# Values loaded uncast by a hardware queue and cast on chip, with weights taking over attention buffers one by one

## The chip, the cores and the metric

One Trainium2 chip, one core. The time is the device time of one execution in microseconds (us), and the figure quoted for a kernel is the median of its runs. Most executions of one kernel agree within 1 to 2%. A run more than 1.5% above the fastest of its kernel counts as slow and stays out of the ratios. GB/s counts the bytes as they land: a float32 to float16 load is counted at half of what it reads.

## The reference

Sliding-window attention for 8 batches of 8 heads (576 rows, 64 columns), then a mixture of experts with 32 soft slots over the 4608 rows of 512.

```python
# attention: heads 0-3 see the last 32 rows, heads 4-7 every fourth of the last 128
scores = scale * np.matmul(q, k.transpose(0, 1, 3, 2))
mask_plain = (rel >= 0) & (rel < 32)
mask_dil = (rel >= 0) & (rel < 128) & (rel % 4 == 0)
attn = softmax(np.where(mask, scores, -1e9)); x = np.matmul(attn, v)
# experts
logits = x @ phi                                  # 4608 x 32
slot_input = softmax(logits, axis=0).T @ x        # 32 x 512
for e in range(8):
    slot_out[e] = np.maximum(slot_input[e] @ w1[e], 0) @ w2[e]
out = softmax(logits, axis=1) @ slot_out          # 4608 x 512
```

The inputs are float32 in HBM. q, k and v are 9.4 MB each, w1 and w2 16.8 MB each, the output 9.4 MB.

## The kernel before

Everything on chip is float16, and every load but two small constants is a cast load issued by GpSimd, so all large loads share one queue and land in the order of issue. A batch takes q and k, the values, and one first-layer weight:

```python
def load_v_plain(b):                       # heads 0-3, six loads of 96 rows
    for t in range(NT):
        nc.gpsimd.dma_start(out=vP[b % NV][32:128, t, :, 0:D],
                            in_=v[b, 0:4, QT * t : QT * t + QT, :].rearrange("h a d -> a h d"))

def load_v_dil(b):                         # heads 4-7: 128 rows, and a left-over block of 48
    nc.gpsimd.dma_start(out=sa, in_=v[b, 4:8, 0:512, :].rearrange("h (a r) d -> a h (r d)", r=DIL))
    nc.gpsimd.dma_start(out=sb[0:48], in_=v[b, 4:8, 384:576, :].rearrange("h (a r) d -> a h (r d)", r=DIL))

# ... in the loop over batches b and steps kt:
            if att and kt == 1:
                if b + 2 < B:
                    load_qk(0, b + 2); load_qk(1, b + 2); load_w1(b)
                # ... b == 6: w1 6, 7 and w2 0, 1;  b == 7: w2 2, 3, 4 into the freed staging space
            if att and kt == 2 and b + 1 < B:
                spread_v_dil(b + 1)        # two GpSimd copies out of sa, sb
            if att and kt == 3 and b + 2 < B:
                load_v_plain(b + 2); load_v_dil(b + 2)
# ... after the loop
    fix.release()                          # all attention buffers at once
    for e in (5, 6, 7):
        load_w2(e, 2 if e == 7 else 1)
```

In these traces an instruction that waits holds up what stands behind it on its engine (below, GpSimd stands 20.7 us in front of a cast and issues its next loads only then). What order that is, a compile-time scheduler decides: it may move an instruction ahead of others on its engine.

The softmax here doesn't subtract the row's maximum and nothing guards it: scores larger than these inputs give would overflow.

## Time and profile before

| | us |
|---|---|
| time, median of 3 runs | 210.29 (208.48 to 213.9) |
| one batch, from one batch's first exponential to the next | about 16.3 |
| batch 7 begins | 124.5 |
| last piece of the slot inputs (`er`) | 153.5 |
| first output issued | 181.8 |
| end of the profiled span | 210.3 |

The profiled run, at 212.0 us, is 0.8% above the median of before.

The page's rows for the engines (busy us, share of the span, instructions; PE is TensorE, PEld its weight loads, DVE VectorE, ACT ScalarE, POOL GpSimd), for the GB/s in 40 slices of 5.3 us, for the two large queues (packets, MB, share), and for the chain that ended last:

```profile
PE 151.5 (72%) x2128; PEld 92.8 (44%) x2128; DVE 134.4 (64%) x346; ACT 84.2 (40%) x134; POOL 105.7 (50%) x156
...
GB/s 112 157 161 207 121 134 210 182 170 210 179 125 210 186 156 209 188 119 210 194 137 211 198 145 208 201 188 207 207 207 208 207 207 127 85 408 402 409 407 91
...
q0 software_dynamic: 47744, 40.94, 116.9%
q1 hardware_dynamic: 288, 0.27, 0.5%
...
## 4 chain that ended last, share of the span: by engine, by line
PE 36%; issue 23%; DVE 13%; DMA 10%; ACT 8%; POOL 7%; POOLq 0%; DVEq 0%
```

No single engine fills the chain. The GB/s row shows a hole in nearly every third slice, down to 119 to 170 beside 210, and then six slices flat at 207 or 208: the DMA wastes time in attention and is the limit afterwards. Almost all packets belong to q0, GpSimd's queue.

The view of waits names the hole (engine and what it was about to do, what it waited for, then total us, times, longest):

```profile
POOL vsb_1325 L159 <- DMA vP_99<-in_v_dram: 5.3, 1, 5.3
POOL vsb_327 L159 <- DMA vP_99<-in_v_dram: 4.9, 1, 4.9
...
PE so L581 <- DMA w_6_3027<-in_moe_w_dram: 3.1, 1, 3.1
```

GpSimd stands 4 to 5 us in front of the eighth value load of a batch. It is in order, so the next batch's q, k and weight are issued late too. The last line is TensorE waiting for a second-layer weight in the tail.

Stretches of the span by window (us, then the busy time of PE, PEld, DVE, ACT and POOL with instruction counts, TensorE's clock, DMA share, GB/s):

```profile
...
75.00:91.00 16.00, 14.77 (x242) 10.09 (x240) 13.50 (x38) 8.62 (x14) 8.70 (x13) 1.00 1.24 182
91.00:107.00 16.00, 14.60 (x241) 10.07 (x240) 13.28 (x37) 8.44 (x14) 9.80 (x13) 1.00 1.23 180
...
140.00:160.00 20.00, 14.34 (x223) 9.40 (x226) 6.69 (x23) 4.92 (x9) 3.25 (x4) 1.00 1.24 206
160.00:180.00 20.00, 13.95 (x108) 5.76 (x101) 1.22 (x3) 1.55 (x3) 0.00 (x0) 0.91 1.04 173
181.00:207.00 26.00, 13.93 (x34) 3.18 (x32) 13.15 (x18) 11.72 (x18) 19.12 (x36) 0.64 1.31 364
```

In the two batches the DMA moved 180 to 182 GB/s, in the weights' backlog 206, in the output 364 over its whole stretch. The last weights' way from issue to landing (KB each, us):

```profile
w_5_3025<-in_moe_w_dram POOLq DMA_DIRECT2D x1, 1024.0 KB, 20.4
...
w_7_3029<-in_moe_w_dram POOLq DMA_DIRECT2D x2, 512.0 KB, 27.1
```

They wait 20 to 27 us for a transfer of 5: the backlog, not the issue, is what they wait for.

### The profile page before, as it was taken

How to read it: one execution, taken by the hardware profiler on the slowest of the kernel's cores; microseconds unless marked ns; L12 is line 12 of the kernel's file. 1: busy time of each engine (PE TensorE's matmuls, PEld its weight loads, DVE VectorE, ACT ScalarE, POOL GpSimd, SP SyncE). 2: the span in 40 equal slices, each digit the busy share in tenths (PEclk: the TensorE clock that was granted, in tenths of full speed). 3: DMA queues.
4: the chain of work that ended last, by engine and by line, in shares of the span. 5: the costliest groups of instructions: out<-in, count | busy, mean ns of one | idle time of the engine just before them, and what ended most of it. 6: DMA issues, size and time to landing. Idle time of an engine off the chain costs nothing.

```text
span 210.3 us, 5183 instructions
## 1 busy us (share of the span) xinstructions
PE 151.5 (72%) x2128; PEld 92.8 (44%) x2128; DVE 134.4 (64%) x346; ACT 84.2 (40%) x134; POOL 105.7 (50%) x156
## 2 busy tenths in 40 slices
PE   0123549899899899899899989977678838775800
PEld 0122436557556557557556656746353512211100
DVE  2685799968878878878879879665320200654620
ACT  2014306536545655655554464562401100653520
POOL 7775597295187196179169176100600000488860
PEclk9999999999999999999999999999999996985555
DMA  6999989999989999999999999999999997399993
GB/s 112 157 161 207 121 134 210 182 170 210 179 125 210 186 156 209 188 119 210 194 137 211 198 145 208 201 188 207 207 207 208 207 207 127 85 408 402 409 407 91
DMA packets 48056, 41.54 MB, mean 198 GB/s; under 512 B 21280, under 2 KB 35232, under 8 KB 48032
## 3 DMA queue, kind: packets, MB, share of 16 engines
q0 software_dynamic: 47744, 40.94, 116.9%
q1 hardware_dynamic: 288, 0.27, 0.5%
q8 instruction: 17, 0.28, 0.5%
q14 instruction: 7, 0.06, 0.1%
HBM read 63.25 MB, written 9.44 MB: 346 GB/s over the span
## 4 chain that ended last, share of the span: by engine, by line
PE 36%; issue 23%; DVE 13%; DMA 10%; ACT 8%; POOL 7%; POOLq 0%; DVEq 0%
DMA raw_1_172<-in_k_dram 6%; POOL out_dram L605 3%; DMA raw_0_135<-in_k_dram 3%; ACT ET L351 2%; DMA out_dram<-ot_3287 2%; DVE vP_98 L172 1%; DVE kTd_92 L197 1%; DVE pd_5_2443 L244 1%; POOL w_7_3029 L181 1%; DVE pd_5_1034 L244 1%; PE s_4_2038 L226 1%; DVE vP_99 L172 1%; DVE qTd_96 L197 1%; PE s_5_2771 L226 1%; DVE kTp_89 L188 1%
## 5 line engine op out<-in xcount | busy, mean ns | idle before, releaser
L605 POOL DMA_DIRECT2D out_dram<-ot_3237 x1 | 0.6, 557 | 30.6 <-ACT ot_3237 L600 30.6
L226 PEld LDWEIGHTS <-kTp_89 32*128 32x128 f16 x192 | 6.7, 121 | 14.4 <-DVE kTp_89 L188 10.4
L147 POOL DMA_DIRECT2D vP_98<-in_v_dram x18 | 12.2, 685 | 1.3 <-DMA vsa_165<-in_v_dram 1.1
L348 PEld LDWEIGHTS <-phi_61 128*128 128x128 f16 x64 | 7.8, 131 | 9.7 <-issue 5.6
L147 POOL DMA_DIRECT2D vP_97<-in_v_dram x18 | 12.0, 678 | 0.0
L226 PEld LDWEIGHTS <-kTd_91 32*128 32x128 f16 x256 | 7.2, 112 | 7.4 <-DVE emask L436 3.7
L597 PEld LDWEIGHTS <-ET 128*128 128x128 f16 x36 | 3.6, 99 | 15.4 <-issue 14.1
L589 DVE CAST so_sb<-so 128x256 f16<-128x256 f32 x1 | 0.4, 425 | 15.3 <-ACT so_sb L588 15.3
L226 PEld LDWEIGHTS <-kTd_92 32*128 32x128 f16 x256 | 7.6, 111 | 4.3 <-issue 2.0
L226 PEld LDWEIGHTS <-kTp_90 32*128 32x128 f16 x192 | 6.9, 122 | 5.6 <-DVE kTp_90 L188 1.8
L181 POOL DMA_DIRECT2D w_5_3025<-in_moe_w_dram x1 | 0.9, 881 | 15.6 <-PE o_10_2919 L292 15.6
L147 POOL DMA_DIRECT2D vP_99<-in_v_dram x12 | 8.0, 677 | 0.0
L226 PE MATMUL s_0_199<-qTp_93,kTp_89 32*128 32x96 f16 x12 | 0.7, 270 | 9.4 <-DVE kTp_89 L188 9.4
L581 PEld LDWEIGHTS <-hTm_3042 128*32 128x32 f16 x32 | 3.0, 103 | 9.8 <-issue 7.4
L588 ACT CAST so_sb<-so 128x256 f16<-128x256 f32 x1 | 0.4, 372 | 14.3 <-PE so L581 14.3
L565 DVE TENSOR_SCALAR h_sb<-hps 128x512 f16<-128x512 f32 x1 | 0.7, 692 | 6.5 <-ACT h_sb L564 6.5
L581 PE MATMUL so<-w_6_3027,hTm_3042 128*32 128x512 f16 x8 | 2.5, 467 | 3.1 <-DMA w_6_3027<-in_moe_w_dram 3.1
L564 ACT ACTIVATE h_sb<-hps 128x512 f16<-128x512 f32 x1 | 0.6, 597 | 9.5 <-PE hps L547 9.5
L362 PEld LDWEIGHTS <-ET 32*128 32x128 f16 x48 | 1.9, 101 | 5.5 <-ACT ET L351 5.5
L393 PEld LDWEIGHTS <-ones 96*128 96x128 f16 x48 | 4.0, 104 | 0.0
L188 DVE STREAM_TRANSPOSE qTp_93<-raw_0_133 128x576 uint32<-128x576 uint32 x1 | 1.3, 1260 | 4.1 <-DMA raw_0_133<-in_q_dram 4.1
L239 ACT ACTIVATE pa_0_212<-s_0_199 128x576 f16<-128x576 f32 x1 | 0.7, 651 | 8.0 <-PE s_0_199 L226 8.0
(1062 smaller groups left out, 625.8 us busy)
## 6 DMA issues: line engine op xcount, KB each, us to landing
w_0_76<-in_moe_w_dram POOLq DMA_DIRECT2D x1, 1024.0 KB, 12.6
w_1_77<-in_moe_w_dram POOLq DMA_DIRECT2D x1, 1024.0 KB, 13.7
w_2_78<-in_moe_w_dram POOLq DMA_DIRECT2D x1, 1024.0 KB, 13.2
w_3_79<-in_moe_w_dram POOLq DMA_DIRECT2D x1, 1024.0 KB, 14.2
w_4_80<-in_moe_w_dram POOLq DMA_DIRECT2D x1, 1024.0 KB, 13.6
w_5_81<-in_moe_w_dram POOLq DMA_DIRECT2D x1, 1024.0 KB, 12.6
w_6_82<-in_moe_w_dram POOLq DMA_DIRECT2D x1, 1024.0 KB, 8.6
w_7_83<-in_moe_w_dram POOLq DMA_DIRECT2D x1, 1024.0 KB, 13.4
```

The source lines that it names most:

```text
L147: nc.gpsimd.dma_start(out=vt[32:128, t, :, 0:D], in_=v[b, 0:4, QT * t : QT * t + QT, :].rearrange("h a d -> a h d"),)
L172: nc.vector.tensor_copy(out=vt[0:32, 1:NT, :, 0:D], in_=vt[96:128, 0 : NT - 1, :, 0:D])
L188: nc.vector.transpose(out=dst, in_=src)
L197: nc.vector.transpose(out=o, in_=i)
L226: nc.tensor.matmul(sps[:, hh, c0 : c0 + w], kt_[p0 : p0 + 32, k0 : k0 + 128, tt], qt_[p0 : p0 + 32, q0 : q0 + w, tt], start=(tt == 0), sto ...
L244: nc.vector.tensor_tensor(out=pt[:, :, 0:n], in0=pt[:, :, 0:n], in1=m[:, None, :].broadcast_to([128, 2, n]), op=ALU.mult,)
L348: nc.tensor.matmul(lp, phi4[:, kc].rearrange("p c s -> p (c s)"), rhs, start=(kc == 0), stop=(kc == 3))
L351: nc.scalar.activation(out=ET[:, b * S : b * S + S].rearrange("p (i r) -> p r i", r=DIL)[:, 2 * rp : 2 * rp + 2, :], in_=lp, func=AF.Exp, ...
L393: nc.tensor.matmul(up[:, c, :], l, rr, start=(i == 0), stop=(i == len(jobs) - 1), skip_group_check=True)
L581: nc.tensor.matmul(so[32 * j : 32 * j + 32, :], hTm[g][:, c, 32 * j : 32 * j + 32], w2t[4 * g + j][:, c, :], start=(g == 0 and c == 0), st ...
L597: nc.tensor.matmul(fp, ET[:, r0 : r0 + 128], so_sb, start=True, stop=True)
L605: nc.gpsimd.dma_start(out=out[r0 : r0 + 128, :], in_=ot)
```

## The change

The intent is to relieve GpSimd's queue. Values go by the hardware queue of SyncE (SP) as float32 and are cast on ScalarE and GpSimd; the left-over block loads only its 16 new rows, and VectorE copies the other 32. Value buffers go from three to two, in slabs as large as a second-layer weight, so that weights can take over the attention buffers one by one instead of after the loop. Two parts, then: the values' way (part A), and the slabs (part B).

```diff
-    NV = 3
+    NV = 2
-    vP = [fix.tile([128, NT, 4, VW], FP16, ...) for i in range(NV)]      # and vD, vL, kTp, kTd, qTp, qTd
+    for i in range(NV):
+        slab = fix.tile([128, V_SLAB], FP16, name=f"v{i}", tag=f"v{i}")  # vP, vD, vL are views; q, k likewise
# ...
+    stage_p = vs_pool.tile([128, NT, 4, D], FP32, name="stage_p", tag="vs")
+    stage_d = vs_pool.tile([128, 4, DIL * D], FP32, name="stage_d", tag="vsd")
+    stage_l = stage_p[0:LEFT, 2:NT].rearrange("p t h d -> p t (h d)")
-    def load_v_plain(b): ...   def load_v_dil(b): ...   def spread_v_dil(b): ...
+    def load_v(b):
+        for t in range(NT):
+            nc.sync.dma_start(out=stage_p[32:128, t, :, :], in_=v[b, 0:4, QT * t : QT * t + QT, :]...)
+        nc.sync.dma_start(out=stage_d, in_=v[b, 4:8, 0:512, :]...)
+        nc.sync.dma_start(out=stage_l, in_=v[b, 4:8, 512:576, :]...)
+    def cast_v_plain(b):  nc.scalar.copy(out=vP[b % NV][:, :, :, 0:D], in_=stage_p)
+    def cast_v_left(b):   nc.gpsimd.tensor_copy(out=vL[b % NV][32 : 32 + LEFT, :, :, 0:D], in_=stage_l...)
+    def cast_v_dil(b):    nc.gpsimd.tensor_copy(out=vD[b % NV][:, :, :, 0:D], in_=stage_d...)
+    def shift_v_left(b):  nc.vector.tensor_copy(out=vL[b % NV][0:32, ...], in_=vD[b % NV][96:128, ...])
# ... in the loop
+            if att and b + 1 < B:
+                if kt == 1:   cast_v_plain(b + 1)
+                elif kt == 3: cast_v_dil(b + 1); cast_v_left(b + 1); load_v(b + 2)   # if b + 2 < B
-                    load_w1(b)
+                    for _ in range((1, 2, 1, 1, 1, 2)[b]): load_w1(next_w1.pop(0))
+                    slab = fix.tile([128, QK_SLAB], FP16, name="w2_6", tag="qk0")    # b == 7: w2_6 into q, k of batch 6
+            if b == B - 1 and kt == 3:
+                slab = fix.tile([128, V_SLAB], FP16, name="w2_7", tag="v0")           # w2_7 into the values of batch 6
-    fix.release()
-    for e in (5, 6, 7): load_w2(e, 2 if e == 7 else 1)
```

There is one float32 staging buffer for each kind of value, shared by all batches: a load can start only when the cast before it is done.

More of the change, by code (lines that the diff above doesn't have):

```diff
@@ L99 @@
     w1t = [w1_pool.tile([128, 4, FDIM], FP16, name=f"w1_{e}", tag=f"w1_{e}") for e in range(E_EXP)]
-    w2t = {e: w2a_pool.tile([128, 8, DMODEL], FP16, name=f"w2_{e}", tag=f"w2_{e}") for e in range(2)}
-    NV = 3
+    w2t = {e: w2a_pool.tile([128, 8, DMODEL], FP16, name=f"w2_{e}", tag=f"w2_{e}") for e in range(3)}
+    NV = 2
     fix = tc.alloc_tile_pool(name="fix", bufs=1)
-    kTp = [fix.tile([128, 32 + S, 2], FP16, name=f"kTp{i}", tag=f"kTp{i}") for i in range(2)]
-    kTd = [fix.tile([128, S + 80, 2], FP16, name=f"kTd{i}", tag=f"kTd{i}") for i in range(2)]
-    qTp = [fix.tile([128, S, 2], FP16, name=f"qTp{i}", tag=f"qTp{i}") for i in range(2)]
-    qTd = [fix.tile([128, S + 16, 2], FP16, name=f"qTd{i}", tag=f"qTd{i}") for i in range(2)]
-    vP = [fix.tile([128, NT, 4, VW], FP16, name=f"vP{i}", tag=f"vP{i}") for i in range(NV)]
-    vD = [fix.tile([128, 4, DIL, VW], FP16, name=f"vD{i}", tag=f"vD{i}") for i in range(NV)]
-    vL = [fix.tile([128, 4, DIL, VW], FP16, name=f"vL{i}", tag=f"vL{i}") for i in range(NV)]
+    QK_SLAB, V_SLAB = 2 * (32 + S + S + 80 + S + S + 16), 4096
+    kTp, kTd, qTp, qTd, vP, vD, vL = [], [], [], [], [], [], []
+    for i in range(2):
+        slab = fix.tile([128, QK_SLAB], FP16, name=f"qk{i}", tag=f"qk{i}")
+        o = 0
+        for dst, n in ((kTp, 32 + S), (kTd, S + 80), (qTp, S), (qTd, S + 16)):
+            dst.append(slab[:, o : o + 2 * n].rearrange("p (s t) -> p s t", t=2))
+            o += 2 * n
+    for i in range(NV):
+        slab = fix.tile([128, V_SLAB], FP16, name=f"v{i}", tag=f"v{i}")
+        o = 0
+        for dst, n in ((vP, NT), (vD, 4), (vL, 4)):
+            dst.append(slab[:, o : o + n * 4 * VW].rearrange("p (a b d) -> p a b d", a=n, b=4))
+            o += n * 4 * VW
     x_pool = tc.alloc_tile_pool(name="xp", bufs=2)
@@ L116 @@
     s_pool = tc.alloc_tile_pool(name="small", bufs=3)
-    vs_pool = tc.alloc_tile_pool(name="vstage", bufs=2, side="right")
+    vs_pool = tc.alloc_tile_pool(name="vstage", bufs=1, side="right")
     raw_pool = tc.alloc_tile_pool(name="raw", bufs=2, side="right")
@@ L125 @@
     raw = {}
-    vstage = {}
+    stage_p = vs_pool.tile([128, NT, 4, D], FP32, name="stage_p", tag="vs")
+    stage_d = vs_pool.tile([128, 4, DIL * D], FP32, name="stage_d", tag="vsd")
+    stage_l = stage_p[0:LEFT, 2:NT].rearrange("p t h d -> p t (h d)")
     def load_qk(ti, b, groups=None):
@@ L142, in load_qk, with cast_v_plain, cast_v_left, cast_v_dil @@
                 )
-    def load_v_plain(b):
-        vt = vP[b % NV]
+    def load_v(b):
         for t in range(NT):
-            nc.gpsimd.dma_start(
-                out=vt[32:128, t, :, 0:D],
+            nc.sync.dma_start(
+                out=stage_p[32:128, t, :, :],
                 in_=v[b, 0:4, QT * t : QT * t + QT, :].rearrange("h a d -> a h d"),
             )
-    def load_v_dil(b):
-        sa = vs_pool.tile([128, 4, DIL * D], FP16, name=f"vsa_{b}", tag="vsa")
-        sb = vs_pool.tile([128, 4, DIL * D], FP16, name=f"vsb_{b}", tag="vsb")
-        vstage[b] = (sa, sb)
-        nc.gpsimd.dma_start(
-            out=sa, in_=v[b, 4:8, 0:512, :].rearrange("h (a r) d -> a h (r d)", r=DIL)
-        )
-        nc.gpsimd.dma_start(
-            out=sb[0:48], in_=v[b, 4:8, 384:576, :].rearrange("h (a r) d -> a h (r d)", r=DIL)
-        )
-    def spread_v_dil(b):
-        sa, sb = vstage.pop(b)
-        for st, dst, n in ((sa, vD[b % NV], 128), (sb, vL[b % NV], 48)):
-            nc.gpsimd.tensor_copy(
-                out=dst[0:n, :, :, 0:D], in_=st[0:n].rearrange("a h (r d) -> a h r d", r=DIL)
-            )
+        nc.sync.dma_start(
+            out=stage_d, in_=v[b, 4:8, 0:512, :].rearrange("h (a r) d -> a h (r d)", r=DIL)
+        )
+        nc.sync.dma_start(
+            out=stage_l,
+            in_=v[b, 4:8, 512:576, :].rearrange("h (a r) d -> a h (r d)", r=DIL),
+        )
+    def cast_v_plain(b):
+        nc.scalar.copy(out=vP[b % NV][:, :, :, 0:D], in_=stage_p)
+    def cast_v_left(b):
+        nc.gpsimd.tensor_copy(
+            out=vL[b % NV][32 : 32 + LEFT, :, :, 0:D],
+            in_=stage_l.rearrange("a h (r d) -> a h r d", r=DIL),
+        )
+    def cast_v_dil(b):
+        nc.gpsimd.tensor_copy(
+            out=vD[b % NV][:, :, :, 0:D],
+            in_=stage_d.rearrange("a h (r d) -> a h r d", r=DIL),
+        )
     def shift_v_plain(b):
@@ L172, in shift_v_plain, with shift_v_left @@
         nc.vector.tensor_copy(out=vt[0:32, 1:NT, :, 0:D], in_=vt[96:128, 0 : NT - 1, :, 0:D])
+    def shift_v_left(b):
+        nc.vector.tensor_copy(out=vL[b % NV][0:32, :, :, 0:D], in_=vD[b % NV][96:128, :, :, 0:D])
     def load_w1(e):
@@ L404 @@
     nc.sync.dma_start(out=masks, in_=masks_dram.ap())
-    nc.sync.dma_start(out=ident, in_=ident_dram.ap())
+    nc.vector.memset(stage_p[0:32], 0.0)
+    load_v(0)
+    nc.scalar.dma_start(out=ident, in_=ident_dram.ap())
     for i in range(2):
@@ L414 @@
         nc.vector.memset(vL[i][:, :, :, D : D + 1], 1.0)
-    load_v_plain(0)
     load_qk(0, 0, (1,))
     load_qk(1, 0, (1,))
-    load_v_dil(0)
     nc.gpsimd.dma_start(out=phi_raw, in_=moe_phi.rearrange("(c p) s -> p c s", p=128))
@@ L421 @@
     load_qk(1, 1)
-    load_v_plain(1)
-    load_v_dil(1)
-    spread_v_dil(0)
+    cast_v_plain(0)
+    cast_v_left(0)
+    cast_v_dil(0)
+    load_v(1)
     qk_plain(0, 0)
@@ L435 @@
         qk_dil(1, 0, part)
+    shift_v_left(0)
     nc.vector.tensor_copy(out=emask[:, NE - 1, :], in_=masks[:, WP + NLEFT + 512 :])
@@ L439 @@
     AV_AT = {0: (5,), 1: (6, 7), 2: (8, 9, 10), 3: (0, 1), 4: (2,), 5: (3, 4)}
+    next_w1 = list(range(E_EXP))
     for b in range(B + 2):
@@ L460 @@
                     qk_dil(1, b + 1, 0)
+                    shift_v_left(b + 1)
             if att and b > 0 and kt == 0:
@@ L483 @@
                     back_u(b2)
+            if att and b + 1 < B:
+                if kt == 1:
+                    cast_v_plain(b + 1)
+                elif kt == 3:
+                    cast_v_dil(b + 1)
+                    cast_v_left(b + 1)
+                    if b + 2 < B:
+                        load_v(b + 2)
             if att and kt == 1:
@@ L488 @@
                     load_qk(1, b + 2)
-                    load_w1(b)
+                    for _ in range((1, 2, 1, 1, 1, 2)[b]):
+                        load_w1(next_w1.pop(0))
                 elif b == 6:
-                    load_w1(6)
-                    load_w1(7)
-                    load_w2(0)
-                    load_w2(1)
+                    for e in range(3):
+                        load_w2(e)
                 else:
@@ L498 @@
                     w2b_pool = tc.alloc_tile_pool(name="w2b", bufs=1, side="right")
-                    for e in (2, 3, 4):
+                    for e in (3, 4, 5):
                         w2t[e] = w2b_pool.tile([128, 8, DMODEL], FP16, name=f"w2_{e}", tag=f"w2_{e}")
                         load_w2(e)
-            if att and kt == 2 and b + 1 < B:
-                spread_v_dil(b + 1)
-            if att and kt == 3 and b + 2 < B:
-                load_v_plain(b + 2)
-                load_v_dil(b + 2)
+                    slab = fix.tile([128, QK_SLAB], FP16, name="w2_6", tag="qk0")
+                    w2t[6] = slab[:, 0 : 8 * DMODEL].rearrange("p (c n) -> p c n", c=8)
+                    load_w2(6)
+            if b == B - 1 and kt == 3:
+                slab = fix.tile([128, V_SLAB], FP16, name="w2_7", tag="v0")
+                w2t[7] = slab.rearrange("p (c n) -> p c n", c=8)
+                load_w2(7, 4)
     psum_o.release()
@@ L513 @@
     x_pool.release()
-    fix.release()
-    w2c_pool = tc.alloc_tile_pool(name="w2c", bufs=1)
-    for e in (5, 6, 7):
-        w2t[e] = w2c_pool.tile([128, 8, DMODEL], FP16, name=f"w2_{e}", tag=f"w2_{e}")
-        load_w2(e, 2 if e == 7 else 1)
     h_pool = tc.alloc_tile_pool(name="hp", bufs=1)
@@ L608 @@
     h_pool.release()
-    w2c_pool.release()
+    fix.release()
     w2b_pool.release()
```

## The prediction

> **What bounds it now.** Three stretches. (1) Attention, to about 148 us: the chain of waits runs through PE, ACT and DVE, with no DMA from about 24 us on; one batch takes 16.3 us (first score matmuls at 58.3, 74.9, 91.0, 107.3, 123.8 us in the timeline), PE about 90% busy. (2) 148 to 180 us: the expert hidden layer is transposed and ready at 164.6, but the last second-layer weights land at 173.3 (w_6) and about 178 (w_7). The five-microsecond windows show 207 GB/s flat from 140 to 175 us: the last seven weights are one DMA backlog, 5.05 us per weight. The late release of the buffers (147.9) costs nothing; w_5, issued then, starts when w_4 has landed. (3) 181.8 to 210: output at 407 GB/s, unchanged by the edit.
>
> The tail's DMA backlog exists because DMA is wasted earlier: windows of 1 us show 45-130 GB/s around 25-29, 58-61, 74-77, where GpSimd sits 4-5 us before the eighth value load (waits: `vsb` after `vP`, 4.1-5.3 us, six times) and issues the next q, k and weight late. I estimate 12 us of idle DMA.
>
> **What changes.** Eight value loads per batch leave GpSimd for SP, as float32: destination packets of 256 B for 128 B; the overlapping 48-row load becomes 16 rows. Added per batch: an ACT cast of 128x1536 (about 1.5 us, from 1.02 for 128x1024), a DVE copy 32x1024 (about 0.4, from 0.48 for 32x1280), the two GpSimd casts stay (about 1.05 each). PE's work is the same.
>
> **What GpSimd's new order does.** Freed, it issues weights far ahead. In the built order ten weights stand before the k load of batch 6 (four before), eleven before batch 7's (five before). They share one first-in-first-out queue. Estimate, at 208 GB/s: ten weights 50.5 us, seven batches of q and k 39.7, six or seven values at about 3.5 (from 2304 packets at 1100/us and the rest) 21-24, start 3: k of batch 6 lands at about 115 (100.8 before), where VectorE transposed it at about 104.5. So batch 6 starts at about 117 instead of 107.3, batch 7 at 133-134 instead of 123.8: attention ends 9 to 10 us later. Against that all second-layer weights are in by about 157, and from hidden layer to `so` takes 9.8 us instead of 15 (1.7 + 4x1.9 us): 5.4 us back. Net about +4 us, plus a little for the ACT cast: 215.
>
> **A risk.** The Trainium skill, "DMA: Bandwidth & Descriptors", Queues, rings and completion order, says that an engine round-robins between queues by packet. This trace shows no such contention. If a 256 B value packet takes turns with a 4 KB weight packet (158 ns each, from 32 packets per engine in 5.05 us), a value load takes 25-30 us beside a full weight queue, ACT blocks on the cast, and the total goes to 225-235.
>
> **Right if:** no value loads on GpSimd, weights landing at a steady 205-210 GB/s from about 3 to 115 us without the dips; batch 1 earlier (about 20 us, 24.6 before); batches 5 and 6 late, VectorE waiting for raw_6; no PE wait on second-layer weights; output stretch still about 28 us.
>
> **Wrong if:** q and k loads are not held up by the weights (then hT at about 160, total near 202); value loads starve (above); the casts on ACT cost a microsecond or more per batch on the chain.
>
> Faster by over 2%: 0.22; within: 0.33; slower: 0.45.

## The result, and the profile after

The changed kernel takes **270.92 us** (269.87 to 272.18, four runs, all fast) beside 210.1 for before (median now of four runs): ratio 1.293, 95% interval 1.2829 to 1.3032. A ratio here is always the mean time of one kernel's fast runs over that of before's fast runs of the same rounds, so not quite the ratio of the medians.

| us | before | after | difference to the stage's start |
|---|---|---|---|
| batch 7 begins | 124.5 | 192.6 | +68.1 |
| last `er` | 153.5 | 219.4 | -2.2 |
| first output issued | 181.8 | 240.2 | -7.5 |
| end of span | 210.3 | 268.1 | -0.6 |

So everything is lost in the attention loop. The batches take 26.5, 26.0, 36.4, 29.0, 25.5, 22.0 and 16.9 us instead of about 16.3. The tail won 7.5 us, as the prediction hoped, and the output is as it was.

The same rows of the page after:

```profile
PE 148.3 (55%) x2128; PEld 91.8 (34%) x2128; DVE 135.3 (50%) x351; ACT 95.1 (35%) x142; POOL 63.5 (24%) x94
...
GB/s 153 193 211 173 120 204 205 142 152 206 203 119 183 208 126 227 206 215 117 192 202 163 131 231 154 125 55 2 117 96 193 206 179 4 0 0 407 408 408 186
...
q0 software_dynamic: 22688, 35.69, 68.3%
q1 hardware_dynamic: 24208, 9.67, 16.7%
...
## 4 chain that ended last, share of the span: by engine, by line
DMA 35%; PE 24%; SPq 15%; issue 9%; ACT 8%; DVE 3%; POOL 2%; POOLq 0%; ACTq 0%
DMA stage_p<-in_v_dram 35%; SPq L157 11%; SPq L161 5%; PE so L607 2%; PE hps L573 2%; POOL out_dram L631 2%; ACT v_92 L170 2%; ACT v_93 L170 2%; ACT ET L368 2%; PE s_5_2413 L243 0%; PE lg_0_2407 L365 0%; PE lg_0_2062 L365 0%; PE s_5_2068 L243 0%; PE s_3_2308 L243 0%; PE s_4_2369 L243 0%
```

TensorE does the same work in a longer span. The values now stand in q1 with 24,208 packets of 400 bytes on average, q0 with 22,688 of 1,570. More than a third of the chain is one kind of transfer, the landing of `stage_p`, and another 15% is SyncE's sequencer (SPq) issuing the value loads.

The costly groups (busy us, mean ns, then idle time of the engine before them and what ended most of it):

```profile
L186 DVE COPY v_92<-v_92 32x1280 f16<-32x1280 f16 x4 | 3.1, 786 | 46.1 <-ACT v_92 L170 46.1
...
L170 ACT CAST v_92<-stage_p 128x1536 f16<-128x1536 f32 x4 | 5.9, 1472 | 47.3 <-DMA stage_p<-in_v_dram 41.3
L179 POOL CAST v_93<-stage_d 128x1024 f16<-128x1024 f32 x4 | 4.1, 1037 | 53.0 <-DMA stage_d<-in_v_dram 34.2
...
L173 POOL CAST v_92<-stage_p 16x1024 f16<-16x1024 f32 x4 | 4.1, 1031 | 36.0 <-DMA stage_p<-in_v_dram 35.9
```

The casts themselves are cheap, 1.47 us on ScalarE and 1.03 on GpSimd. In front of them the engines stand: in the batches that use value buffer `v_92`, ScalarE 47 us, VectorE 46 and GpSimd 36 (line L173); in those of `v_93`, GpSimd 53 us (line L179).

The chain, piece by piece for the first three batches (start us, us, what):

```profile
8.36 17.59 DMA stage_p<-in_v_dram
26.01 1.48 ACT v_92 L170
...
32.15 19.66 DMA stage_p<-in_v_dram
51.87 1.48 ACT v_93 L170
...
56.82 4.37 SPq L161
61.29 16.11 DMA stage_p<-in_v_dram
77.47 1.48 ACT v_92 L170
```

Each turn is the same: 16 to 20 us from a value load's last issue to its landing, a cast, the next batch's load issued a few us later. In all the chain has six such landings, 17.6 + 19.7 + 16.1 + 12.8 + 11.7 + 16.0 = 93.9 us. Counted from the first issue of a load to its landing, the first three take 24.8, 24.3 and 24.0 us: SyncE's issue is stretched too, with single issues of up to 6.9 us. Why they are, the runs don't show.

What GpSimd did between two of them:

```profile
53.77 0.70 POOL L143 DMA_DIRECT2D raw_3_459<-in_q_dram  x1
...
55.17 0.76 POOL L192 DMA_DIRECT2D w_3_79<-in_moe_w_dram  x1
55.90 0.77 POOL L192 DMA_DIRECT2D w_4_80<-in_moe_w_dram  x1
77.35 1.04 POOL L179 CAST v_92<-stage_d 128x1024 f16<-128x1024 f32 x1 [20.68 <-DMA stage_d<-in_v_dram]
...
79.43 0.71 POOL L143 DMA_DIRECT2D raw_4_815<-in_q_dram  x1
```

It issued q, k and two weights in 3 us, then stood 20.7 us until `stage_d` was in: the casts are in its line too, and what comes behind them, the next q, k and weights, waits. The first of the two weights was in 14.4 us after its issue and the second 19.6, by about 75.5; the values, issued from 53.4 us on, were in at 77.4, as soon as the queue beside them had run dry.

The windows after:

```profile
62.00:99.00 37.00, 19.34 (x285) 12.78 (x281) 16.89 (x45) 13.79 (x22) 5.55 (x7) 1.00 0.90 177
99.00:128.00 29.00, 12.97 (x211) 8.88 (x210) 12.85 (x37) 9.76 (x16) 6.61 (x8) 1.00 0.95 185
...
175.00:192.00 17.00, 15.72 (x247) 10.26 (x248) 14.67 (x39) 9.80 (x15) 2.95 (x3) 1.00 0.16 27
...
220.00:240.00 20.00, 16.21 (x204) 7.92 (x201) 4.03 (x10) 2.38 (x5) 0.00 (x0) 1.00 0.02 4
240.00:266.00 26.00, 13.03 (x32) 2.87 (x29) 12.54 (x18) 11.11 (x17) 19.05 (x36) 0.66 1.31 363
```

The DMA is no faster in the loop, and then it idles: 27 GB/s from 175 to 192 us, where the weights still to come go into space that attention holds, and their issue stands behind GpSimd's last casts (183.5 and 185.0 us, the next weight 187.8); and 4 GB/s from 220 to 240, where all weights are in (the last at 222) and no output is ready. The gain of the tail is just this: when compute is 66 us late, the weights are in.

The trace's packet records show why a value load takes so long. In each microsecond in which values and one other kind of load both move, I counted their packets (means over 12 to 35 such microseconds of each kernel):

| kernel | value packets | beside | value packets per us | others per us |
|---|---|---|---|---|
| after | 256 B | weights, 2048 B | 73 | 88 |
| after | 256 B | q, k, 2304 B | 86 | 78 |
| after | 256 B | nothing | 447 | |
| e2 (below) | 256 B | weights, 2048 B | 74 | 87 |
| e3 (below) | 256 B | weights, 512 B | 221 | 234 |
| e5 (below) | 1536 B | weights, 2048 B | 50 | 71 |

Packets of the two queues go roughly one for one (0.7 to 1.1), whatever their size. The means depend on which microseconds are taken, and some of these also hold 1024 B value packets, which are not counted. By the median of the microseconds with more than five packets of each kind and at most two of any other, it is 86 beside 88 in after, 237 beside 239 in e3 and 70 beside 71 in e5. A batch's plain values are 6 x 96 x 4 = 2304 rows and as many packets of 256 B; by estimate, at 73 per us they last 31.6 us beside weights, at 447 alone 5.2 us.

### The profile page after: what moved, and what is told of

It reads as the page before. It is cut to its first block, busy times and chain, and to the rows that moved or that the text cites. A ratio compares the mean times of both kernels' runs of the same rounds, so it can differ in the third digit from the quotient of the medians.

```text
span 268.1 us, 5176 instructions
## 1 busy us (share of the span) xinstructions
PE 148.3 (55%) x2128; PEld 91.8 (34%) x2128; DVE 135.3 (50%) x351; ACT 95.1 (35%) x142; POOL 63.5 (24%) x94
## 3 DMA queue, kind: packets, MB, share of 16 engines
q0 software_dynamic: 22688, 35.69, 68.3%
q1 hardware_dynamic: 24208, 9.67, 16.7%
## 4 chain that ended last, share of the span: by engine, by line
DMA 35%; PE 24%; SPq 15%; issue 9%; ACT 8%; DVE 3%; POOL 2%; POOLq 0%; ACTq 0%
DMA stage_p<-in_v_dram 35%; SPq L157 11%; SPq L161 5%; PE so L607 2%; PE hps L573 2%; POOL out_dram L631 2%; ACT v_92 L170 2%; ACT v_93 L170 2%; ACT ET L368 2%; PE s_5_2413 L243 0%; PE lg_0_2407 L365 0%; PE lg_0_2062 L365 0%; PE s_5_2068 L243 0%; PE s_3_2308 L243 0%; PE s_4_2369 L243 0%
## 5 line engine op out<-in xcount | busy, mean ns | idle before, releaser
L186 DVE COPY v_92<-v_92 32x1280 f16<-32x1280 f16 x4 | 3.1, 786 | 46.1 <-ACT v_92 L170 46.1
L243 PEld LDWEIGHTS <-qk_91 32*128 32x128 f16 x448 | 14.7, 115 | 31.3 <-issue 26.3
L170 ACT CAST v_92<-stage_p 128x1536 f16<-128x1536 f32 x4 | 5.9, 1472 | 47.3 <-DMA stage_p<-in_v_dram 41.3
L179 POOL CAST v_93<-stage_d 128x1024 f16<-128x1024 f32 x4 | 4.1, 1037 | 53.0 <-DMA stage_d<-in_v_dram 34.2
L170 ACT CAST v_93<-stage_p 128x1536 f16<-128x1536 f32 x4 | 5.9, 1470 | 28.8 <-DMA stage_p<-in_v_dram 28.8
L186 DVE COPY v_93<-v_93 32x1280 f16<-32x1280 f16 x4 | 2.5, 637 | 22.8 <-ACT v_93 L170 22.6
L173 POOL CAST v_92<-stage_p 16x1024 f16<-16x1024 f32 x4 | 4.1, 1031 | 36.0 <-DMA stage_p<-in_v_dram 35.9
L243 PE MATMUL s_2_221<-qk_90 32*128 32x96 f16 (+2 forms) x28 | 1.1, 215 | 19.6 <-DVE qk_90 L214 19.0
L179 POOL CAST v_92<-stage_d 128x1024 f16<-128x1024 f32 x4 | 4.1, 1034 | 30.4 <-DMA stage_d<-in_v_dram 28.0
L365 PE MATMUL lg_0_1351<-xTp_1122,phi_61 128*128 128x288 f16 x2 | 0.7, 425 | 14.6 <-ACT xTd_1294 L353 14.6
L243 PE MATMUL s_4_603<-qk_91 32*128 32x128 f16 x16 | 1.3, 297 | 12.6 <-ACT pb_2_494 L256 12.6
L243 PE MATMUL s_2_820<-qk_90 32*128 32x96 f16 (+2 forms) x28 | 1.3, 215 | 11.8 <-DVE qk_90 L214 11.8
L173 POOL CAST v_93<-stage_p 16x1024 f16<-16x1024 f32 x4 | 4.3, 1064 | 10.0 <-DMA stage_p<-in_v_dram 9.4
L278 PE MATMUL o_1_1641<-v_92,pa_0_1415 128*128 128x65 f16 x2 | 0.3, 240 | 10.2 <-DVE xd_1461 L320 10.2
L243 PE MATMUL s_0_184<-qk_90 32*128 32x96 f16 x12 | 0.7, 271 | 9.5 <-DVE qk_90 L205 9.5
L189 DVE COPY v_93<-v_93 32x1024 f16<-32x1024 f16 x4 | 1.9, 478 | 6.0 <-POOL v_93 L179 5.9
L243 PE MATMUL s_5_2068<-qk_91 32*128 32x128 f16 x16 | 1.3, 297 | 5.7 <-ACT pb_3_1984 L256 5.7
L573 PE MATMUL hps<-w_0_76,siTm 128*32 128x512 f16 x8 | 3.6, 610 | 1.0 <-DVE siTm L559 1.0
## 6 DMA issues: line engine op xcount, KB each, us to landing
w_0_76<-in_moe_w_dram POOLq DMA_DIRECT2D x1, 1024.0 KB, 19.7
w_3_79<-in_moe_w_dram POOLq DMA_DIRECT2D x1, 1024.0 KB, 14.4
w_4_80<-in_moe_w_dram POOLq DMA_DIRECT2D x1, 1024.0 KB, 19.6
```

The source lines that it names most:

```text
L170: nc.scalar.copy(out=vP[b % NV][:, :, :, 0:D], in_=stage_p)
L173: nc.gpsimd.tensor_copy(out=vL[b % NV][32 : 32 + LEFT, :, :, 0:D], in_=stage_l.rearrange("a h (r d) -> a h r d", r=DIL),)
L179: nc.gpsimd.tensor_copy(out=vD[b % NV][:, :, :, 0:D], in_=stage_d.rearrange("a h (r d) -> a h r d", r=DIL),)
L186: nc.vector.tensor_copy(out=vt[0:32, 1:NT, :, 0:D], in_=vt[96:128, 0 : NT - 1, :, 0:D])
L243: nc.tensor.matmul(sps[:, hh, c0 : c0 + w], kt_[p0 : p0 + 32, k0 : k0 + 128, tt], qt_[p0 : p0 + 32, q0 : q0 + w, tt], start=(tt == 0), sto ...
L365: nc.tensor.matmul(lp, phi4[:, kc].rearrange("p c s -> p (c s)"), rhs, start=(kc == 0), stop=(kc == 3))
```

## The experiments

The kernels ran with runs of before beside them: 210.11 us in e1, e2, e3 and e5, 210.53 in e6 to e9, 210.40 in e10 to e13. My theory was the turn-taking: a 256 B packet gets the same number of turns as a 2 to 4 KB packet, so a value load lasts until GpSimd's queue is empty, and in-order casts hand the delay on. The rivals: SyncE's queue is slow at small packets by itself; the casts cost too much on chip; the single staging buffer serialises; the new buffers and weight schedule of part B do harm. Landmarks of all profiled runs, in us:

| run | batch 7 begins | last `er` | first output | span |
|---|---|---|---|---|
| e1 | 141.5 | 172.5 | 193.8 | 221.0 |
| e2 | 163.9 | 190.8 | 211.2 | 239.1 |
| e3 | 179.2 | 205.7 | 228.7 | 257.0 |
| e5 | 147.1 | 173.6 | 194.7 | 222.6 |
| e6 | 125.7 | 153.9 | 182.8 | 211.5 |
| e7 | 121.2 | 148.2 | 169.0 | 196.4 |
| e8 | 161.4 | 187.9 | 208.3 | 236.2 |
| e9 | 152.2 | 175.7 | 195.3 | 222.4 |
| e10 | 138.3 | 164.4 | 184.8 | 211.9 |
| e11 | 120.9 | 147.2 | 166.7 | 193.9 |
| e12 | 119.5 | 148.7 | 174.4 | 202.5 |

### e1: the same uncast loads, on GpSimd's queue

```diff
-            nc.sync.dma_start(      # all three kinds of value load
+            nc.gpsimd.dma_start(
```

> Theories. Turns: a 256 B value packet on the SP queue waits for a whole q, k or weight packet of the GpSimd queue at every turn, so a value load lasts as long as that queue is full. Slow queue: the SP queue is slow for 256 B packets by itself. Staging: the single float32 staging buffer and the casts on ACT and GpSimd, which stand in order ahead of other work, cost the time, whatever the queue. Here the values are still uncast, staged and cast on chip, but issued from GpSimd. Turns and slow queue expect 205 to 222 us and batches of 16 to 18 us; staging expects 255 to 275 us, as after.

Measured: 222.22 us (221.29 to 222.72), ratio 1.0566, interval 1.0501 to 1.0632, correct. So 48.7 of the 60.8 us go when the same float32 bytes, casts and buffers use the other queue. The total is just above the range I had named for turns, and the batches missed it: five of seven take 19.7 to 21.1 us, not 16 to 18. That leaves about 12 us, and this line of the waits says where GpSimd now stands:

```profile
POOL stage_p L157 <- ACT v L170: 49.1, 6, 10.1
```

Six times about 8 us, for ScalarE to free the one staging buffer. One thing was unexpected: through GpSimd the uncast values travel in 1920 packets of 4096 B and 768 of 2048 B; on SyncE's queue the same rows were 18,432 packets of 256 B and 4,608 of 1024 B. So e1 changes the size of the packets along with the queue.

### e2: weights held at their place in the program

```diff
-        nc.gpsimd.dma_start(out=w1t[e], in_=...)
+        tc.keep_in_program_order(nc.gpsimd.dma_start(out=w1t[e], in_=...))   # w2 likewise
```

> Weights are pinned behind the q and k loads that stand before them in the program, instead of running up to six weights ahead; values stay on SP. Turns: per batch 64 packets per engine (10.7 us) stand beside the values instead of up to 128, so a value load takes about 14 us, a batch about 18 us, total 225 to 240 us. If issuing weights ahead has no part in it (staging, slow queue): 262 to 275 us.

Measured: 244.44 us (240.85 to 247.01; two of four runs fast), ratio 1.1628, interval 1.151 to 1.1746, correct. A queue that holds less takes fewer turns, and 28.9 us go between the means of the fast runs (26.5 between the medians). Even the two fast runs (240.85 and 243.25) lie a little above the range I had named. The steps are 22.5 to 26.0 us for the first three batches, 17.1, 16.3 and 16.9 for three in the middle, and 31.3 again for the last, where a value load took 30 us from its first issue (122.7) to its landing (152.8).

### e3: weights in 512 B packets

```diff
-        nc.gpsimd.dma_start(out=w1t[e], in_=moe_w1[e].rearrange("(c p) f -> p c f", p=128))
+        for i in range(4):        # four column pieces
+            nc.gpsimd.dma_start(out=w1t[e][:, :, 256 * i : 256 * i + 256], in_=src1[:, :, 256 * i : 256 * i + 256])
```

> First-layer weights are loaded in four column pieces, so their packets are 512 B at the destination for 2048 B, same bytes, values untouched. Turns: each turn of a value packet against a weight costs about 40 ns for 158, a value load about 13 us for 18 to 22 in the first six batches, total 230 to 250 us; in the trace, per us beside weights, about 250 to 350 value packets for 88. Slow queue and staging: value loads as slow as after, total 262 to 280 us.

Measured: 257.08 us (two runs), ratio 1.2229, interval 1.209 to 1.2369, correct. The total is outside what I expected, and so is the packet rate (221, not 250 to 350); the q and k packets and the second-layer weights were left as they were, the landings of `stage_p` are still 35% of the chain, and what else holds it I did not follow up. The turn itself behaves as the theory says: with a quarter of the packet size beside them the values get 221 packets per us instead of 73, again one for one. A queue that is slow by itself would have stayed at 73.

### e5: the values in six times larger packets (wrong rows on purpose)

```diff
-        for t in range(NT):
-            nc.sync.dma_start(out=stage_p[32:128, t, :, :], in_=v[b, 0:4, QT * t : QT * t + QT, :].rearrange("h a d -> a h d"))
+        nc.sync.dma_start(out=stage_p[32:128].rearrange("p h t d -> p h (t d)"),
+                          in_=v[b, 0:4].rearrange("h (a t) d -> a h (t d)", t=NT))
```

A partition takes six consecutive rows, so the result is wrong (relative error 0.319), while bytes, casts and engines are the same.

> WRONG RESULT ON PURPOSE: the plain values are loaded with six neighbouring rows in one run (1536 B packets, 384 of them in one load, for 2304 of 256 B in six loads), same bytes, same queue, same weights ahead. Turns: a value load needs some 60 turns per engine for 176, about 10 us; total 215 to 235 us. Slow queue (so many packets per us): improves too, to 220 to 240. Staging and casts: 262 to 275 us.

Measured: 224.87 us (two runs), ratio 1.0697, interval 1.0604 to 1.079. Same queue, same bytes, larger packets: 46 us less. Six loads became one as well, so some of it may be SyncE's issue: it is 0% of this run's chain, 15% in after. The ranges for turns and for a slow queue overlap here, so e3 is what tells them apart. The packet table shows 50 packets of 1536 B per us, 77 GB/s, where 73 of 256 B are 19.

### e6: part B alone

```diff
 # the kernel before, with its own value loads, and NV = 3
+    QK_SLAB, V_SLAB slabs; load_w1 by (1, 2, 1, 1, 1, 2)
+    w2_6 into "qk0"; w2_5 into "v2" at b == 6 and w2_7 into "v0" at b == 7, kt == 3
-    fix.release(); w2_5, w2_6, w2_7 after the loop
```

> Only the second half of the change: value loads exactly as before (cast by the DMA, GpSimd queue, three buffers), one first-layer weight more in batch 1, second-layer weights into attention buffers as these come free (w2_5 in a value buffer, w2_6 in the q/k buffer, w2_7 in a value buffer). My reading of before: the last weights were held by the DMA backlog, not by the late release; so only the one weight moved forward counts (5 us): 203 to 209 us. If this half carried part of the loss (weights ahead of q and k): 213 to 225. If the late release had been the cost: 196 to 203.

Measured: 211.58 us (209.87 to 213.24; the profiled run is a slow one), ratio 1.0029, interval 0.9943 to 1.0114, correct. Part B does no harm, and it wins nothing: I had expected 5 us, and the median lies between the ranges I had named. Two points differ from the change: three value buffers, and `w2_5` goes into one of them. The last weight lands at 179.5 us here and at 178.1 in before. An earlier issue only makes a backlog longer.

### e8: two staging buffers, values still on SyncE's queue

```diff
-    stage_p = vs_pool.tile([128, NT, 4, D], FP32, name="stage_p", tag="vs")
+    stages_p = [vs_pool.tile([128, NT, 4, D], FP32, ...) for i in range(2)]   # stage_d likewise; w2_2 waits for the space
+                    load_v(b + 2)      # now at kt == 1, ahead of q and k
```

> As after (values on SP), but with two float32 staging buffers and each value load issued as soon as its buffer is free, a batch earlier. Turns: packets still alternate one for one, so a value load still takes 15 to 25 us beside a full weight queue, but most of it passes before the cast needs it: 225 to 245 us. If turns alone count and nothing is hidden: 262 to 275. If the single buffer was the whole cause: 208 to 218.

Measured: 238.36 us (235.78 to 243.42; three of four fast), ratio 1.1288, interval 1.1181 to 1.1394, correct. The steps are 30.7, 24.1 and 33.1 us for the first three batches, and then 15.8 four times, less than before's 16.3, with all casts and copies in place. ScalarE's casts in this run:

```profile
L170 ACT CAST v<-stage_p x8: 1472/1472/1472, 27.1 to 149.1; 128x1536 f16<-128x1536 f32 x8
...
  DMA stage_p<-in_v_dram: 42.7, 3
```

Eight casts of 1472 ns, and only three of them waited for their values. So the casts do not cost a batch anything when the values are there. They are late in the first batches, where both queues are full.

### e9: two staging buffers on GpSimd's queue

> As e1_v_on_pool (values uncast on the GpSimd queue, 222 us), with two staging buffers. There GpSimd stood 8 to 10 us per batch before a value load, waiting for the ACT cast to free the one buffer, with q, k and weights behind it. If that is the rest of the loss: 205 to 214 us. If the casts and copies on ACT and VectorE are: 218 to 224.

This is e1 with e8's edit. Measured: 224.33 us (224.15 to 224.44), ratio 1.0661, interval 1.0594 to 1.0727, correct. GpSimd's wait for ScalarE fell from 49.1 to 2.6 us, and the time did not fall. Part of the wait only moved: GpSimd now stands 16.3 us in four waits before the eighth value load, up to 4.9 us each, as in before. I had expected that then the casts are to blame, but e8 had run the same casts at 15.8 us a batch, and the trace of e9 shows the loads early: batch 5's values were in at 88 and its q and k at 93.7 us, and the batch began at 112.6. VectorE shows why:

```profile
107.78 0.48 DVE L186 COPY v<-v 32x1280 f16<-32x1280 f16 x1
108.30 1.26 DVE L205 STREAM_TRANSPOSE qk<-raw 128x576 uint32<-128x576 uint32 x1
109.40 0.71 DVE L214 STREAM_TRANSPOSE qk<-raw 128x320 uint32<-128x320 uint32 x1
...
110.19 0.59 DVE L214 STREAM_TRANSPOSE qk<-raw 128x256 uint32<-128x256 uint32 x1
110.64 1.22 DVE L205 STREAM_TRANSPOSE qk<-raw 128x576 uint32<-128x576 uint32 x1
111.70 1.38 DVE L214 STREAM_TRANSPOSE qk<-raw 128x320 uint32<-128x320 uint32 x2
```

At compile time the scheduler had put the whole block of batch 5's q and k transposes and one of the two value copies behind nearly everything of batch 4, directly in front of batch 5's first scores, where TensorE has to wait for it (35.1 us in eight such waits over the run). In before, in e1 and in e8 two of the six transposes come 6 to 20 us earlier than the next batch's first exponential; here all six stand in the last 4.3 us.

### e10 and e13: e9 with the program's order held

```diff
+    class Pinned: ...               # wraps an engine: every instruction goes through tc.keep_in_program_order
+    dve = Pinned(nc.vector)         # e13: ScalarE and TensorE as well
-        nc.vector.transpose(out=dst, in_=src)
+        dve.transpose(out=dst, in_=src)      # and all of VectorE's others in the batch loop
```

> The kernel with two staging buffers and uncast values on the GpSimd queue, with nothing changed but that VectorE keeps the order of the program in the batch loop; the compile-time scheduler had put all of the next batch's q and k transposes in one block behind the current batch, in front of the next batch's first scores. If that order is what holds it at 224 us (its loads for batch 5 had landed 19 us before batch 5 began), the batch steps fall from about 20 us to 16 to 17.5 and the time to 203 to 213 us, where the weights' landing takes over. If the twice as many value bytes on the DMA hold it, nothing changes: steps of 20 us and 220 to 226 us.

> The same with TensorE and ScalarE held in program order as well. If the order on VectorE is the whole of it, within 3 us of the run with VectorE alone held; if TensorE's or ScalarE's order matters too, 4 us or more off in either direction.

Measured: e10 213.39 us (212.98 to 215.49), ratio 1.0153, interval 1.0095 to 1.021; e13 212.63 us (two runs), ratio 1.0096, interval 1.0051 to 1.0142; both correct. The order on VectorE was worth 10.9 us of medians, and the other engines add less than a microsecond. e10 lies 0.4 us above the range I had named. Its steps are 16.8 to 18.7 us after a first one of 24.6. In this form, with GpSimd's queue, two buffers and the program's order, the changed kernel is 1.5% slower than before. The hole before the eighth value load is in it again:

```profile
POOL stage_p L183 <- DMA stage_p<-in_v_dram: 23.4, 5, 4.8
```

This form with fewer loads was not run.

### e7: before's way of loading values, with fewer loads

The hole before each eighth value load (shown above) was still there to be had. e7 is e6 with four plain loads, one for each head, in place of six, and with the 16 new rows of the left-over block alone, cast by the DMA.

```diff
-        for t in range(NT):
-            nc.gpsimd.dma_start(out=vt[32:128, t, :, 0:D], in_=v[b, 0:4, QT * t : QT * t + QT, :].rearrange("h a d -> a h d"))
+        for h in range(4):
+            nc.gpsimd.dma_start(out=vt[32:128, :, h, 0:D], in_=v[b, h].rearrange("(t a) d -> a t d", t=NT))
-            out=sb[0:48], in_=v[b, 4:8, 384:576, :]...
+            out=sb[32:48], in_=v[b, 4:8, 512:576, :]...
+        nc.vector.tensor_copy(out=vL[b % NV][0:32, :, :, 0:D], in_=vD[b % NV][96:128, :, :, 0:D])
```

> As e6_slabs_only, and the values in six DMAs for eight (one per head for one per 96 rows; 16 new rows of the left-over block for 48, the rest shifted on VectorE). If the idle DMA of before comes from GpSimd standing before the eighth value load, the dips to 45-130 GB/s shrink, weights land earlier, and the hidden layer (not the weights) sets the tail: 199 to 206 us. If the DMA's idle time is not what sets the end: like e6, within 1%.

Measured (VectorE copies the other 32 rows): **196.85 us** (196.26 to 198.2), ratio 0.9364, interval 0.9295 to 0.9434, correct. It beats both kernels, and by more than I expected. Two batches in the windows, to hold against those of before:

```profile
74.00:90.00 16.00, 14.66 (x240) 10.18 (x240) 14.16 (x38) 8.60 (x16) 10.76 (x15) 1.00 1.30 203
90.00:106.00 16.00, 14.42 (x241) 10.22 (x242) 14.97 (x40) 8.90 (x16) 9.73 (x14) 1.00 1.30 199
```

TensorE's busy time is the same and the DMA moves 199 to 203 GB/s instead of 180 to 182. GpSimd's wait before the last value load is nearly gone; all that its waits still hold in front of it is this:

```profile
POOL vsb L166 <- DMA raw<-in_k_dram: 0.7, 1, 0.7
```

Before weights it still stands 9.5 us in three waits. The last weight lands at 160.2 us instead of 178.1.

### e11 and e12: e7 without its parts

```diff
 # e11: before (no slabs) with e7's value loads
 # e12: e7 with before's six plain loads
```

> The kernel before with the smaller, fewer value loads of the 196.9 us version, but without the weights in the attention buffers: the last three second-layer weights are issued only when attention has ended. If the buffers handed over matter once the DMA keeps up, three weights of about 5 us each land after about 149 us and the first output is issued 3 to 5 us later than in the 196.9 us version: 199 to 203 us. If they don't matter: 196 to 198 us.

> The weights in the attention buffers and six plain value loads per batch as before, but only the 16 new rows of the left-over block loaded and the rest shifted on VectorE: half of what made the 196.9 us version. If the number of plain loads is what counts, 207 to 212 us; if the rows loaded twice are, 197 to 201 us; if both count alike, 202 to 206 us.

Measured: e11 **195.51 us** (194.59 to 196.61), ratio 0.9284, interval 0.9231 to 0.9338; e12 207.05 us (204.22 to 207.13), ratio 0.9799, interval 0.9731 to 0.9866; both correct. Without the slabs it is no slower, so part B wins nothing even where the DMA keeps up: the space of the last weights came free while the last batch's back end still ran (they were issued at 141.6 us) and all had landed at 162.9, four microseconds before the first output. e11 missed both of my ranges, on the good side. e12 keeps the hole:

```profile
POOL vsb L166 <- DMA w<-in_moe_w_dram: 13.3, 3, 5.0
POOL vsb L166 <- DMA v<-in_v_dram: 13.2, 3, 4.4
```

With six plain loads, GpSimd waits before the last value load as in before, 26.5 us in six waits, and the gain is 2%; with four it is 6.4%. So the number of loads makes most of it (10.2 us from e12 to e7), and the rows that are not loaded twice make the rest (4.5 us from e6 to e12, across two calls). The plain values are 18,432 packets of 128 B in before, e7 and e12 alike, so it is not the packets' number or size. e7 also loads by head where e12 loads by stretches of rows; that order was not tried by itself.

## Why the prediction was wrong

The call was 215 us, or 225 to 235 if the named risk came true; it is 270.92, beyond both.

- **The failed step is the term "six or seven values at about 3.5" us in the first-in-first-out estimate.** It priced a value load as if its packets passed at 1100 per us. In fact 73 per us passed beside weights and 447 alone, and a value load lasted about as long as GpSimd's queue had anything in it: 24 to 25 us from its first issue in the first three batches, of which 16 to 20 after its last; 93.9 us of these landings are on the chain. e1 shows the size, 48.7 us for the other queue with its larger packets, and e3, e5 and the packet counts show that it is turns by packet.
- **The mechanism was in the prediction, as "a risk".** It put 25 to 30 us on a value load beside a full queue. From the counts it is 31.6 us for the plain part; from issue to landing it was 24 us for the load issued at 53.4, whose first packets moved before q and k did (402 and 342 in its first two microseconds). It was then carried into a total of only 225 to 235 and given less weight than the estimate that ignored it. What was left out is that the wait comes back every batch: one staging buffer ties the next load to the cast, and ScalarE and GpSimd, in order, stand behind it. e2 and e8 take away the fuller queue or the single buffer, and each gets back some 29 to 34 us (means of fast runs).
- **"Freed, it issues weights far ahead" failed with it.** Ten weights do stand before batch 6's k load in the order of issue, as predicted. But GpSimd was not free: the casts stood in its line, and it issued two weights and then waited 20.7 us. So no steady 205 GB/s, and DMA idle at 175 to 192 us.
- **"Batch 1 earlier"** failed: its first exponential ran at 36.7 us instead of 25.3.
- **The casts** were priced right, 1.47 us for "about 1.5" and 0.48 for "about 0.4", and e8 shows that a batch with them can take 15.8 us. They cost nothing that shows there; they block because they wait.
- **The tail's numbers were right, by luck**: no TensorE wait on second-layer weights, 20.8 us from the last `er` to the first output instead of 28.3, output still about 28 us. But the reason given, all second-layer weights in by about 157, failed: the last is in at 222. Compute was 66 us late and needed them later still. e6 and e11 add that the buffers handed over have no part in it.
- **The reading of before was right, and worth more than the change**: the hole before the eighth value load, estimated at "12 us of idle DMA", is 10.2 of the 13.7 us that e7 wins; the rest are the rows not loaded twice.

What stays open: of e1's 12 us, the single buffer and the scheduler's order make 9 together, but their single shares are not known, since taking away the one brought in the other (I did not run e1 with its order held). Two value buffers in place of three were not tried alone; e10 and e13, which have two, lose 1.0 to 1.5% to before with everything in. What makes the hole before the eighth value load, why single issues on SyncE stretch to 6.9 us, and why GpSimd's queue joined rows that SyncE's did not, the runs do not say.

## What to carry to other kernels

Before a load is moved to a second queue, count its packets and those of the queue beside it: here they took turns by packet (73 to 86 beside 88 per us), so 256 B packets beside 2048 B ones got a small share of the bandwidth (19 to 22 GB/s) for as long as the other queue was full. Anything in order behind that load, a cast or a later issue, waited with it, batch after batch. And look first for what the old queue wastes: fewer and larger loads on the same queue won here what the second queue was meant to win.

## What the Trainium skill lacked or had wrong

- "DMA: Bandwidth & Descriptors", Queues, rings and completion order: it says that an engine takes turns between queues by packet, "≈9-17 descriptors typical" in each. The trace agrees with the turns (73 value packets beside 88 weight packets per us). It lacks what that makes of a bandwidth share, and here a value packet, as the trace records it, held one row of 256 B: 19 GB/s for the values, where 1536 B packets got 77. Whether the page means the same packets, the runs do not say.
- The same page, Issuing engines are not separate DMA queues: that issuing from several engines "will only save the time on the sequencer" misses what it can cost. With the same loads the kernel took 222.2 us from GpSimd and 270.9 from SyncE.
- The same page, Issuing engine by pattern: "HWDGE (sync/scalar) is generally faster" did not hold for these 256 B rows beside a full GpSimd queue (same numbers).
- The same page, SWDGE vs HWDGE vs iDMA: it names packets of preferably at most 4096 B for GpSimd's loads. Most of the uncast values did go in 4096 B (1920 packets, 7.9 MB, 30 us if their durations are spread over the 16 DMA engines), but the cast ones in packets of 128 B (18,432 packets, 2.4 MB, 37 us). No page that I read says that a cast load's rows are not joined.
- No page that I read has GpSimd's wait of 4 to 5 us before the eighth value load of a batch, which went when the plain loads fell from six to four (e7 beside e12: 10.2 us).
